# Attention on 64x64 TensorE tiles: 60-key tiles, stationary V, and a normaliser by Ln and Exp

## The chip, the cores and the metric

The kernel runs on one core of a Trainium2 chip. The time is the device time of one execution in microseconds; of three runs of the kernel before, the median is 182.83 (182.55 to 184.69).

A core has four engines that matter here, each with its own in-order queue: TensorE (PE in the profile; PEld is its weight load) multiplies matrices and writes to PSUM, VectorE (DVE) and ScalarE (ACT) work on elements, GpSimd (POOL) makes tables and issues DMAs, and SyncE (SP) issues DMAs. PSUM has eight banks here; a group of matmuls fills one or two, and DVE or ACT empties them before the next group can have them.

## The reference

Attention with a window, then a gated long convolution. B = 4, H = 8 heads, S = 768, D = 64, so 512 model columns.

```python
scores = scale * np.matmul(q, k.transpose(0, 1, 3, 2))
is_global = pos[None, :] < 8
is_local = (rel >= 0) & (rel < 96)                   # rel = query - key
keep = is_global | is_local
bias = -slopes[:, None, None] * dist                 # dist: 96 for far global keys
a = softmax(where(keep, scores + bias, -1e9))
x = (a @ v) as (B, S, 512)
proj = x @ w_proj                                    # x1, x2, x3, 512 columns each
x2_conv = irfft(rfft(x2) * rfft(filter), n=768)
out = (x1 * x2_conv * x3) @ w_out
```

Every query sees itself, the 95 keys before it, and the first eight keys.

## The kernel before

The kernel is one long program over four batches. `attention(b)` makes x transposed (`xT`, model columns on partitions), `gate` multiplies it with the outer two thirds of w_proj (L910), `conv(b)` does the middle third (L964), a Fourier transform as matmuls (L737), the product with the filter's spectrum on DVE, the inverse (L986, L989), the gating and the output projection (L1012).

**How attention is tiled.** Keys are in seven tiles of 120, each of 128 partitions with the eight global keys in front. A tile is seen by 216 queries (the last two by fewer). `transposes` brings q and k, 128 rows at a time, into `QT` and `KT` (L751). `scores` takes a pair of heads: each head's 64 rows of KT and QT are a 64-row tile of TensorE, and the two heads go to two banks (L788). ACT takes Exp of 864 columns at a time (L802), and DVE multiplies with a table of decayed and masked weights (L809); in batch 0, for two of three groups, the distances are instead added in PSUM by matmuls with `near` and `slope` (L779). `values` takes 128 columns of E as the stationary operand and 65 columns of V as the moving one, the 65th a column of ones, so that the row sums come with the result (L827, L832). The result has queries on partitions; DVE takes the reciprocal (L856) and multiplies (L851), and `transpose_x` turns it (L872) and copies it to `xT`.

**What sets the order.** A planner (`Plan`) places every operation on its engine by list scheduling: an operation's rank is its batch's due time plus a bias and a noise, costs are estimates, PSUM banks are given out as the plan goes, and an operation with two possible engines (`"AV"`) takes the earlier one. The order found is written out as the program; at run time the queues follow it and wait by semaphores. `fill` puts matmuls on an unused tile (`busy`, L419) where the plan leaves PE idle. The `table` of an ACT operation tells the planner when to add 1.3 us for a change of activation table. Batch b+1's attention is planned into the time of batch b's convolution. Loads are issued by POOL in 256-byte rows, cast to half precision on the way (L439); batch 0's q comes through SP in full precision and is cast by ACT or DVE. The SP queue also copies the global rows of V and stores the output (L1020).

Of the kernel before, what the change touches and what calls it, by code (L numbers as in the profile page):

```python
# [17 lines left out]
P = 128  # L18
NG = 8
KL = P - NG  # L20
# [40 lines left out]
class Op:  # L61
    __slots__ = ("cost", "fn", "preds", "succs", "wait", "tail", "bias", "acq", "use", "n",
                 "start", "end", "ready", "rank", "noise", "lean", "need", "eng", "bytes", "batch", "table", "name", "order", "first", "landed")


class Plan:
# [7 lines left out]
    def op(self, eng, cost, fn, r=(), w=(), acq=(), use=(), nbytes=0, table=None, name="",  # L74
           bias=0.0, after=()):
# [5 lines left out]
        o.batch, o.bias, o.n = self.batch, self.bias + bias, len(self.ops)  # L81
# [69 lines left out]
    def schedule(self):  # L151
        self.prepare()
        for seed in self.SEEDS:
            self.shake(seed)
        return self.program(self.fill(self.lay()))

    def shake(self, seed):
        r = random.Random(seed)
        if r.random() < 0.4:
            groups = sorted({(o.name, o.batch) for o in self.ops if o.eng not in "GS"})  # L160
            g, by = r.choice(groups), r.gauss(0.0, 5.0)
            lean = r.gauss(0.0, 0.3)
            for o in self.ops:
                if (o.name, o.batch) == g:
                    o.noise += by
                    o.lean += lean
            return
        share = r.choice((0.005, 0.02, 0.05))
        for o in self.ops:
            if r.random() < share:  # L170
                o.noise += r.gauss(0.0, 5.0)
                o.lean += r.gauss(0.0, 0.3)

    def lay(self):
# [8 lines left out]
        table = [None]  # L183
# [4 lines left out]
        while live:  # L188
# [25 lines left out]
            if e == "A" and o.table and table[0] != o.table:  # L214
                cost += 1.3
                table[0] = o.table
            o.start, o.eng, o.end = s, e, s + cost
# [21 lines left out]
            for x in o.succs + after.get(o, []):  # L239
# [8 lines left out]
    SEEDS = (4, 6, 12, 14, 28, 33, 52, 54, 91, 94, 109, 172, 179, 217, 284, 340, 370, 416, 512,  # L248
             1076, 1771, 1829, 3912, 4133, 4161)
    FAVOUR = 0.0  # L250
# [78 lines left out]
class Fused:  # L329
    PERIOD = 40.0  # L330
    NEAR = 2
    TWICE = frozenset((b, j, s) for b in range(4) for j in range(4) for s in range(2))
    LATER = ()
    WL = [], [], [], [(0, 256), (1024, 256), (256, 256), (1280, 256), (512, 512)]
    SHIFT = 0.0
    LONG = 0.6
    EW = [216, 216, 216, 216, 216, 168, 48]
    GRP = [(0, 1), (2, 3), (4, 5, 6)]
    Q0 = [0, 240, 480]
    QW = [240, 240, 288]  # L340

    def __init__(self, ctx, tc, q, k, v, n_global, n_local, w_proj, filt, w_out, out):
# [10 lines left out]
        self.K0 = [KL * t for t in range(6)] + [S - KL]  # L353
# [6 lines left out]
    def buffers(self):  # L360
# [5 lines left out]
        self.qn = t("qn", [P, 6, H, D])  # L366
        self.kn = t("kn", [P, 7, H, D])
        self.vn = [t(f"vn{i}", [P, 7, H, D + 1]) for i in range(2)]
        self.QT = t("QT", [P, 4, S])
        self.KT = t("KT", [P, 4, 7 * P])  # L370
        self.E = [t(f"E{i}", [P, 2, 1536]) for i in range(4)]
        self.mask = t("mask", [P, H, 648])
        self.xn = [t(f"xn{i}", [P, 2, 7, 2, D]) for i in range(2)]
# [25 lines left out]
        self.rc = [t(f"rc{i}", [P, 12], F32) for i in range(4)]  # L399
        self.dg = t("dg", [P, 264], BF16)  # L400
        self.far = t("far", [NG, 216])
        self.near = t("near", [P, 2, 480], BF16)
        self.slope = t("slope", [P, 4, 2, P], BF16)
# [4 lines left out]
        self.irow = t("irow", [1, 5, P], I32)  # L408
# [27 lines left out]
    def load(self, eng, dst, src, w, nbytes, name, r=()):  # L436
        self.loads += 1
        e = {"G": self.nc.gpsimd, "S": self.nc.sync}[eng]
        return self.g.op(eng, 0.57 + 0.00035 * nbytes[0] if eng == "G" else 0.5, lambda _: e.dma_start(dst, src),  # L439
                         w=w, r=r, nbytes=nbytes, name=name, bias=-2000.0 + self.loads)  # L440

    def load_rows(self, what, dst, src, b, t):

        lo, hi = self.K0[t], self.K0[t] + KL
        self.load("G", dst[P - (hi - lo):P, t, :, 0:self.D],
                  src[b, :, lo:hi, :].rearrange("h p d -> p h d"), [what + (t,)], (8 * (hi - lo), 256),
                  f"load{what}{t}")

    def load_run(self, what, dst, src, t, n):

        rows = src[0, :, self.K0[t]:self.K0[t] + KL * n, :].rearrange("h (t p) d -> p t h d", t=n)
        self.load("G", dst[NG:P, t:t + n, :, 0:self.D], rows, [what + (i,) for i in range(t, t + n)],
                  (8 * KL * n, 256), f"load{what}{t}")

    def load_q(self, b, t):
        src = self.q[b, :, P * t:P * t + P, :].rearrange("h p d -> p h d")
        if b == 0:
            st = self.ot[t].rearrange("p (h d) -> p h d", h=self.H)
            self.load("S", st, src, [("ot", t)], (1024, 256), f"q{t}")
            self.g.op("AV", {"A": act(512), "V": 0.7}, lambda e: self.copy(  # L460
                e, self.qn[:, t], st), r=[("ot", t)], w=[("qn", t)], name="cast")
        else:
            self.load("G", self.qn[:, t], src, [("qn", t)], (1024, 256), f"q{t}")

    def load_v(self, b, ts):
        vt, s = self.vn[b % 2], b % 2
        if b == 1 and ts[0] == 0:
            self.g.op("V", 0.2, lambda _: self.nc.vector.memset(vt[:, :, :, self.D:], 1.0),
                      w=[("vn1", s)], name="ones")
        for t in ts:  # L470
            self.load_rows(("vn", s), vt, self.v, b, t)
            if t == 0:
                self.load_global(vt, s)

    def load_global(self, vt, s):
        for c, (t, n) in enumerate(((0, 2), (2, 5))):
            self.load("S", vt[0:NG, t:t + n], vt[NG:2 * NG, 0:1].to_broadcast(
                [NG, n, self.H, self.D + 1]), [("vng", s, c)], (8 * n, 1040), "vglobal",
                r=[("vn", s, 0), ("vn1", s)])
# [7 lines left out]
    def setup(self):  # L487
# [4 lines left out]
        g.op("A", 0.2, lambda _: nc.scalar.activation(self.warm, self.warm, Act.Exp),  # L492
             r=["warm"], w=["warm"], table="exp", bias=-4000)
        def irow(_):
            p.iota(self.irow[:, 0:4], pattern=[[1, 4], [6, P]], base=0, channel_multiplier=0)
            p.iota(self.irow[:, 4], pattern=[[1, P]], base=0, channel_multiplier=0)
        g.op("G", 0.8, irow, w=["irow"], bias=-1975.0)

        def rows(_):
            v.memset(self.one, 1.0)  # L500
            for j in range(3):
                v.memset(self.cst[:, j:j + 1], 192.0 * (j + 1))
            v.tensor_copy(self.row, self.irow)
        g.op("V", 0.8, rows, r=["irow"], w=["rows"], bias=-1970)
# [3 lines left out]
        g.op("G", 0.45, ident, w=["ident"], bias=-1998.5)  # L508
        for lo, hi in ((0, 2), (2, 7)):
            g.op("V", dve(512 * (hi - lo), 4), lambda _, lo=lo, hi=hi: v.memset(self.kn[0:NG, lo:hi], 0.0),  # L510
                 w=[("kz", t) for t in range(lo, hi)], bias=-4500 if lo == 0 else -3500)
        for i in range(4):
            et = self.E[i]

            def gaps(_, et=et):
                gap = et[:, :, 0:1488].rearrange("p h (m w) -> p h m w", m=6)[:, :, :, 216:248]
                v.memset(gap, 0.0)
                v.memset(et[:, :, 1456:1536], 1.0)
            g.op("V", 0.34, gaps, w=[("E", i, c) for c in range(3)], name="gaps", bias=-3300)

    def tables(self):

        nc, g, S = self.nc, self.g, self.S
        exps = [x for x in g.ops if x.name in ("exp", "mask")]
        nf = 2.0 * math.pi / S * (1.0 - 4.0e-7)
        for a, n in enumerate((512, 256)):
            b = g.bank()
            g.op("P", 0.5 if a == 0 else 0.3, lambda _, a=a, b=b: self.angles(a, b.f32()),
                 r=["rows"], acq=[b], after=[x for x in exps if x.name == "exp"][7:8], name="angles")
# [11 lines left out]
                 r=[("th", a)], w=[("fwd", a)], table="sin", name="sines", after=exps)  # L541
# [43 lines left out]
    def distances(self):  # L585


        g, nc, NL, n = self.g, self.nc, self.NL, 216
        o = 720 - (self.S - KL)
        p, v, dg, far, mask = nc.gpsimd, nc.vector, self.dg, self.far, self.mask  # L590

        def first(_):
            for ap, w, base in ((dg[:, 0:n], n, NG), (dg[:, n:n + 48], 48, NG + o)):
                p.iota(ap, pattern=[[-1, w]], base=-base, channel_multiplier=1,
                       allow_small_or_imprecise_dtypes=True)
                for sgn, off in ((1, 0), (-1, NL - 1)):
                    if w == 48 and sgn < 0:
                        continue
                    p.affine_select(ap, ap, pattern=[[sgn, w]], base=off + sgn * base,
                                    channel_multiplier=-sgn, compare_op=Alu.is_ge, fill=-HUGE)  # L600
            p.affine_select(dg[:, n:n + 48], dg[:, n:n + 48], pattern=[[0, 48]],
                            base=-NG - o, channel_multiplier=1, compare_op=Alu.is_ge, fill=-HUGE)
# [623 lines left out]
```

## Time and profile before

| | |
|---|---|
| median of three runs | 182.83 us (182.55 to 184.69) |
| span of the profiled execution, first to last instruction | 181.1 us |
| PE busy | 170.5 us, mean granted clock 0.986 |
| DVE busy | 160.4 us |
| ACT busy | 154.1 us |
| POOL busy | 76.5 us |
| gates of batch 0, first matmul to last | 28.58 to 42.85 |
| first gate matmul of batches 1, 2, 3 | 65.04, 103.35, 140.54 |
| last output matmul fed | 177.4 |

The page has only the span of the execution that it shows; what lies around it is not in it, so the table has the runs' times beside it. Busy time is the time in which at least one instruction of an engine was under way. On PE, matmuls overlap, so how much an engine could still take is better read from the distance between starts; on ACT and DVE neighbours overlap by some 0.1 us too.

### The profile page before, as it was taken

How to read it: one execution, taken by the hardware profiler on the slowest of the kernel's cores; microseconds unless marked ns; L12 is line 12 of the kernel's file. 1: busy time of each engine (PE TensorE's matmuls, PEld its weight loads, DVE VectorE, ACT ScalarE, POOL GpSimd, SP SyncE). 2: the span in 40 equal slices, each digit the busy share in tenths (PEclk: the TensorE clock that was granted, in tenths of full speed). 3: DMA queues.
4: the chain of work that ended last, by engine and by line, in shares of the span. 5: the costliest groups of instructions: out<-in, count | busy, mean ns of one | idle time of the engine just before them, and what ended most of it. 6: DMA issues, size and time to landing. Idle time of an engine off the chain costs nothing.

```text
span 181.1 us, 4437 instructions
## 1 busy us (share of the span) xinstructions
PE 170.5 (94%) x1693; PEld 104.6 (58%) x1693; DVE 160.4 (89%) x376; ACT 154.1 (85%) x305; POOL 76.5 (42%) x97
## 2 busy tenths in 40 slices
PE   7895999999879999999999999999999999999991
PEld 2364866666445557974355759654476875447540
DVE  6828779999999999899979989999889999999960
ACT  7885899899999997797998998999789977887652
POOL 7997985279997979999400100000000000000000
PEclk9997899999999999999999999999999999999998
DMA  6999999999999999999963400000440000025135
GB/s 128 202 152 143 138 189 207 180 141 142 143 144 161 151 134 139 139 145 151 143 234 120 31 0 4 0 0 4 174 176 4 0 5 0 0 98 195 58 148 199
DMA packets 90916, 20.47 MB, mean 113 GB/s; under 512 B 83816, under 2 KB 87824, under 8 KB 90896
## 3 DMA queue, kind: packets, MB, share of 16 engines
q0 software_dynamic: 80912, 12.14, 106.4%
q1 hardware_dynamic: 9984, 8.06, 14.3%
q8 instruction: 13, 0.21, 0.5%
q14 instruction: 7, 0.06, 0.1%
HBM read 25.84 MB, written 6.29 MB: 177 GB/s over the span
## 4 chain that ended last, share of the span: by engine, by line
PE 73%; DMA 11%; ACT 7%; POOL 4%; issue 2%; DVE 1%; POOLq 0%; ACTq 0%
PE bank L910 20%; PE bank L1012 12%; PE bank L964 10%; DMA qn<-in_q_dram 7%; PE bank L737 5%; PE bank L751 5%; PE bank L986 5%; PE bank L788 4%; DMA kn<-in_k_dram 4%; PE bank L872 3%; PE bank L827 3%; ACT E L802 3%; PE bank L832 2%; POOL vn L439 1%; ACT h L427 1%
## 5 line engine op out<-in xcount | busy, mean ns | idle before, releaser
L910 PE MATMUL bank<-xT,w 128*128 128x384 f16 x256 | 43.9, 326 | 0.0
L802 ACT ACTIVATE E<-bank 128x864 f16<-128x864 f32 x48 | 41.4, 919 | 0.8 <-PE bank L788 0.4
L910 PEld LDWEIGHTS <-w 128*128 128x128 f16 x256 | 24.2, 98 | 15.4 <-DVE xT L423 0.2
L439 POOL DMA_DIRECT2D kn<-in_k_dram x28 | 25.8, 927 | 11.6 <-PE bank L751 11.4
L439 POOL DMA_DIRECT2D vn<-in_v_dram x28 | 25.8, 927 | 4.3 <-DMA vn<-in_v_dram 1.3
L809 DVE TENSOR_TENSOR E<-E,mask 128x864 f16<-128x864 f16 x40 | 23.1, 596 | 0.5 <-ACT E L802 0.5
L1012 PE MATMUL bank<-wo,y 128*128 128x512 f16 x96 | 21.9, 379 | 0.0
L439 POOL DMA_DIRECT2D qn<-in_q_dram x18 | 16.3, 912 | 6.7 <-ACT fwd L540 3.2
L851 DVE TENSOR_TENSOR xn<-bank,rc 128x512 f16<-128x512 f32 (+1 forms) x24 | 18.3, 770 | 0.3
L920 ACT CAST g<-bank 128x384 f16<-128x384 f32 x32 | 15.7, 496 | 3.2 <-PE bank L910 2.7
L827 PE MATMUL bank<-vn,E 128*128 128x65 f16 x224 | 16.1, 195 | 1.7 <-ACT E L802 1.1
L427 ACT ACTIVATE ot<-bank 128x512 f32<-128x512 f32 x22 | 12.9, 608 | 5.2 <-PE bank L1012 5.1
L827 PEld LDWEIGHTS <-E 128*128 128x128 f16 x224 | 14.5, 98 | 3.9 <-issue 1.0
L788 PE MATMUL bank<-QT,KT 64*128 64x216 f16 (+2 forms) x224 | 15.7, 242 | 1.0 <-ACT E L802 0.7
L427 ACT ACTIVATE ab<-bank 128x512 f16<-128x512 f32 x23 | 14.0, 613 | 2.8 <-PE bank L964 2.8
L427 ACT ACTIVATE x<-bank 128x384 f16<-128x384 f32 x27 | 13.7, 513 | 3.1 <-PE bank L910 2.7
L832 PE MATMUL bank<-vn,E 128*128 128x65 f16 x192 | 15.6, 194 | 0.0
L1012 PEld LDWEIGHTS <-y 128*128 128x128 f16 x96 | 9.2, 98 | 10.7 <-DVE y L1056 0.6
L423 ACT CAST eo<-bank 128x384 f16<-128x384 f32 x28 | 12.0, 513 | 2.8 <-PE bank L989 2.6
L832 PEld LDWEIGHTS <-E 128*128 128x128 f16 x192 | 13.4, 98 | 1.3 <-issue 0.7
L788 PEld LDWEIGHTS <-KT 64*128 64x128 f16 x224 | 8.4, 94 | 9.7 <-issue 6.9
L419 PE MATMUL bank<-idle 128*128 128x512 f16 x37 | 11.9, 452 | 1.2 <-DVE idle L490 1.2
(139 smaller groups left out, 363.0 us busy)
## 6 DMA issues: line engine op xcount, KB each, us to landing
out_dram<-ot SPq DMA_DIRECT2D x24, 256.0 KB, 2.0
kn<-in_k_dram POOLq DMA_DIRECT2D x28, 120.0 KB, 6.0
vn<-in_v_dram POOLq DMA_DIRECT2D x28, 120.0 KB, 7.0
qn<-in_q_dram POOLq DMA_DIRECT2D x18, 128.0 KB, 6.6
ot<-in_q_dram SPq DMA_DIRECT2D x6, 256.0 KB, 6.8
w<-in_moe_w_proj_dram POOLq DMA_DIRECT2D x4, 256.0 KB, 8.0
g<-in_moe_filter_fft_dram POOLq DMA_DIRECT2D x1, 768.0 KB, 13.6
w<-in_moe_w_proj_dram POOLq DMA_DIRECT2D x1, 512.0 KB, 10.6
```

Source lines behind the costliest of these rows:

```text
L427: self.nc.scalar.mul(out, in_, c)
L439: return self.g.op(eng, 0.57 + 0.00035 * nbytes[0] if eng == "G" else 0.5, lambda _: e.dma_start(dst, src), w=w, r=r, nbytes=nbytes, name= ...
L788: nc.tensor.matmul(bs[hh].f32()[:, off:off + w], self.KT[hs, hp, P * m:P * m + P], self.QT[hs, hp, KL * m:KL * m + w], start=(off == 0 and ...
L802: g.op("A", act(864), lambda _: nc.scalar.activation(eo, bs[0].two()[:, :, 0:432].rearrange("p h (m w) -> p h m w", m=2), Act.Exp, scale=s ...
L809: g.op("V", dve(864, 2), lambda _: nc.vector.tensor_mul(eo, eo, mk), r=[("E", hp, gi), ("mask", hp)], w=[("E", hp, gi)], name="masked")
L827: nc.tensor.matmul(o[:, n, hh], ef[:, at:at + P], vt[:, t, 2 * hp + hh, :], start=first, stop=(t == 0), skip_group_check=True)
L832: nc.tensor.matmul(o[:, n, hh], ef[:, at:at + P], vt[:, t - 1, 2 * hp + hh, :], start=False, stop=True, skip_group_check=True)
L851: nc.vector.tensor_mul(to, o[:, :, :, 0:D], rc.to_broadcast([P, 2, 2 * nt, D]))
L910: nc.tensor.matmul(bk.f32()[:, 0:h], self.w[:, c, o + P * j:o + P * j + P], self.xT[:, c, h * s:h * s + h], start=(c == 0), stop=(c == 3))
L920: g.op("A", act(h), lambda _: nc.scalar.copy(x3, pts[1].f32()[:, 0:h]), use=[pts[1]], w=[ko], name="x3")
L964: nc.tensor.matmul(bk.f32(), src[:, c], w[:, c, DM:2 * DM], start=(c == 0), stop=(c == 3))
L1012: nc.tensor.matmul(bk.f32(), y[:, c, P * t:P * t + P], self.wo[:, c, :], start=(c == 0), stop=(c == 3))
```

## The change

**Tiles.** Keys are in 13 tiles of 60, with four global keys in front: 64 partitions, seen by 156 queries. Even tiles hold the first four global keys, odd ones the other four; any two neighbours cover all eight. A pair of heads stands on partitions 0 to 63 and 64 to 127; every score matmul is a 64x64 tile, and the four tiles of TensorE are used by four matmuls in a row: two pairs of heads (banks `bs[0]`, `bs[1]`), two heads each. In one bank, one head's result goes to the upper and the other's to the lower partitions. ACT's Exp takes 936 columns at a time, eight times a batch in place of twelve.

**Values.** V (60 or 64 keys by 64 columns) is stationary and E moves, so the result has model columns on partitions: x comes out transposed, and `transpose_x`, the ones column, the reciprocal and xn are gone.

**Normaliser.** Sums over keys come from matmuls with `ones` in 32-column tiles (`norms`), for queries 0 to 359 and 360 to 767. ACT takes Ln of them and Exp of minus that; both are planned as of table "exp". The result, one row per head, is spread over 64 partitions: in batch 0 by matmuls with `pick` and a copy, afterwards by SP DMAs, eight per half. One DVE multiplication from PSUM gives `xT`.

**Batch 0 and setup.** q and k of batch 0 are loaded by POOL, two heads at a time, six rows of one head behind each other (1536 bytes), and transposed in 64-column tiles. All scores of batch 0 get their distances by matmul. The angle tables for the Fourier transform come first, ahead of attention, and the masks move behind it. V is loaded by half and pair of heads, 60 rows at a time.

**Planner.** PE operations get a mode, and a change of mode costs 0.1 us in the plan; noise and preference are read from two strings, one character per operation, in place of seeds.

The core of the diff:

```diff
 class Fused:
-    EW = [216, 216, 216, 216, 216, 168, 48]
-    GRP = [(0, 1), (2, 3), (4, 5, 6)]
+    SPLIT = 360
+    RUNS = (0, 1, 2), (3, 4, 5), (6, 7, 8), (9, 10, 11, 12)
+    OFF = 0, WIN, 2 * WIN, 2 * WIN + 108
...
+    def load_six(self, what, dst, src, hp):
+        rows = src[0, 2 * hp:2 * hp + 2].rearrange("h (p j) d -> p h (j d)", j=6)
...
+    def scores(self, j, a, near):
...
+            for m, o in zip(self.RUNS[a], self.OFF):
+                w = self.width[m]
+                for i in range(2):
+                    for x in range(2):
+                        hp, hs = 2 * j + i, slice(64 * x, 64 * x + 64)
+                        os = slice(64 * (x ^ i), 64 * (x ^ i) + 64)
+                        nc.tensor.matmul(bs[i].f32()[os, o:o + w], self.KT[hs, hp, m],
+                                         self.QT[hs, hp, KB * m:KB * m + w], start=not near, stop=True,
+                                         skip_group_check=True)
...
+    def norms(self, b, s):
...
+            for i, (m, o, a, c) in enumerate(parts):
+                for hp in range(4):
+                    nc.tensor.matmul(bk.f32()[32 * hp:32 * hp + 32, o], self.ones[:, hp % 2],
+                                     self.E[hp // 2][:, a, hp % 2, c], start=(i == 0),
+                                     stop=(i == len(parts) - 1), skip_group_check=True)
...
+        g.op("A", act(n), lambda _: nc.scalar.activation(ln, bk.f32()[:, 0:n], Act.Ln), use=[bk],
+             w=["ln"], table="exp", name="ln")
+        g.op("A", act(n), lambda _: nc.scalar.activation(r, ln, Act.Exp, scale=-1.0), r=["ln"],
+             w=[("r", s)], table="exp", name="inv den")
+        for hp in range(4):
+            if b == 0:
+                b2 = g.bank()
+                g.op("P", pe(n), lambda _, hp=hp, b2=b2: nc.tensor.matmul(
+                    b2.f32()[:, 0:n], self.pick[:, hp], r, start=True, stop=True), acq=[b2],
+                    r=[("r", s), "pick"], name="spread r")
+                g.op("AV", self.evac(n), lambda e, hp=hp, b2=b2: self.copy(
+                    e, self.rb[:, hp, lo:lo + n], b2.f32()[:, 0:n]), use=[b2], w=[("rb", hp, s)],
+                    name="rb")
+                continue
+            for x in range(2):
+                p0 = 32 * hp + 16 * x
+                self.load("S", self.rb[64 * x:64 * x + 64, hp, lo:lo + n],
+                          r[p0:p0 + 1, None, :].to_broadcast([1, 64, n]),
+                    [("rb", hp, s, x)], (64, 2 * n), "rb", r=[("r", s)])
+
+    def values(self, b, j, s):
...
+            for t, (m, o, a, c) in enumerate(parts):
+                for i in range(2):
+                    for x in range(2):
+                        ks, os = slice(64 * (x ^ i), 64 * (x ^ i) + 64), slice(64 * x, 64 * x + 64)
+                        nc.tensor.matmul(bs[i].f32()[os, o], vt[ks, m, 2 * j + i],
+                                         self.E[j][ks, a, i, c], start=(t == 0),
+                                         stop=(t == len(parts) - 1), skip_group_check=True)
...
+        g.op("V", dve(2 * n, 1, True), lambda _: nc.vector.tensor_mul(
+            self.xT[:, 2 * j:2 * j + 2, lo:lo + n], bs[0].two()[:, :, 0:n],
+            self.rb[:, 2 * j:2 * j + 2, lo:lo + n]), use=bs,
...
-        g.op("V", 0.066 + 0.025 * nt, lambda _: nc.vector.reciprocal(rc, view()[:, :, :, D:D + 1]),
-             use=bs, w=[key], name="rc")
...
-    def transpose_x(self, j, c):
```

## The prediction

> **What bounds the kernel now.** I read the busy shares first (three engines near full; the store's 2.0 us to landing is for later), then the stretches between the gate matmuls (L910) of one batch and the next, then the spacing of matmuls in the timeline and in the chain that ended last.
>
> ```profile
> PE 170.5 (94%) x1693; PEld 104.6 (58%) x1693; DVE 160.4 (89%) x376; ACT 154.1 (85%) x305; POOL 76.5 (42%) x97
> ...
> out_dram<-ot SPq DMA_DIRECT2D x24, 256.0 KB, 2.0
> ```
> Stretches between first gates of batches 1, 2 and 3 and to the end (length, busy time and number of PE, weight loads, DVE, ACT, POOL; clock, DMA share, GB/s): PE, DVE and ACT are all nearly covered, at full clock.
> ```profile
> 65.04:103.35 38.31, 37.96 (x408) 24.38 (x405) 36.09 (x75) 33.15 (x62) 23.01 (x26) 1.00 1.89 140
> 103.35:140.54 37.19, 37.15 (x389) 22.89 (x386) 34.05 (x71) 33.87 (x65) 0.00 (x0) 1.00 0.12 44
> 140.54:177.40 36.86, 36.77 (x279) 21.65 (x275) 33.98 (x76) 27.80 (x57) 0.00 (x0) 1.00 0.18 68
> ```
> The chain (start, length, what): runs of equal matmuls back to back give their spacing.
> ```profile
> 77.06 1.12 PE bank L751 x20
> 78.18 5.20 PE bank L910 x32
> ...
> 140.05 0.56 PE bank L788 x12
> ```
> The timeline (start, length to the end of the last): starts are what counts.
> ```profile
> 124.83 0.38 PE L964 MATMUL bank<-w,xo 128*128 128x512 f16 x1
> 125.14 0.36 PE L788 MATMUL bank<-QT,KT 64*128 64x216 f16 x4
> 125.43 0.60 PE L737 MATMUL bank<-ab,fwd 128*128 128x512 f16 x2
> ...
> 137.38 0.19 PE L827 MATMUL bank<-vn,E 128*128 128x65 f16 x1
> 137.41 0.19 PE L832 MATMUL bank<-vn,E 128*128 128x65 f16 x1
> ```
> A group (busy, mean ns) of 64-column tiles:
> ```profile
> L713 PE MATMUL bank<-g,fwd 128*64 128x512 f16 x8 | 1.1, 385 | 0.0
> ```
> ACT's timeline: spacing of the Exps, and a table load with what follows it.
> ```profile
> 12.25 3.24 ACT L802 ACTIVATE E<-bank 128x864 f16<-128x864 f32 x4
> ...
> 34.37 1.28 ACT L540 ACT_TABLE_LOAD   x1
> 35.66 0.94 ACT L540 ACTIVATE fwd<-y 128x512 f16<-128x512 f32 x2
> ```
> A busy PE is not a full PE (matmuls overlap), so I count spacings. 32 gates in 5.20 us: 162.5 ns for 384 columns, 0.423 ns a column. 20 transposes in 1.12 us: 56 ns. A values matmul, 65 columns: 30 ns, although its own duration is 190. Twelve score matmuls of 1728 columns would need 0.73 us in a row and took 0.56: two 64-row tiles run at once. Eight of 512 columns into 64-column tiles would need 1.7 us and took 1.1: column tiles pair too. Entering and leaving a tiled mode costs 0.1 us each: the 512-column matmul of 124.83 is done feeding at 125.05, the next starts at 125.14; four of 216 feed in 0.18 us, the next starts 0.29 later.
>
> With these prices PE needs 141.2 us from the first gate (28.58) to the last matmul (feeding until 177.4), and 148.9 passed. By stage, elapsed against PE's need: 36.5 to 31.7 (DVE, counted in the same way, needs 35.1 there), 38.3 to 37.4, 37.2 to 36.6, 36.9 to 35.5. **After the first stage PE is full, with DVE (35 to 36) close behind**; the three last stages lose 2.9 us together.
>
> **The change, engine by engine** (counts from the order of the built program).
>
> PE, four batches. Removed: 208 transposes of q and k (11.6 us), 48 slope matmuls (2.9), 224 scores (9.0), 416 values (12.4), 112 transposes of x (6.2), 67 mode changes (6.4): 48.5. Added: 144 transposes whole and 96 half-wide in pairs (10.8), slopes (1.6), 416 scores of 64x64 tiles, 59904 columns, four at once with 10 ns of stagger (7.3), 240 normaliser matmuls in 32-column tiles, four at once (3.7), 8 that spread r (1.3), 480 values (7.4), 77 mode changes (7.3): 39.4. **PE saves 9.1 us.** Four at once is not in the trace; the bounds are that (0) and pairs alone, as the rows show for either tiling (+16.3 for slopes, scores, values). I take four, since row and column pairing each show starts close together.
>
> [...]
>
> ACT, at the spacing of instructions in a row (864-element Exp: 0.77 us; 512: 0.48; 384: 0.37): 48 Exps become 32 of 936 at 0.83 (-10.4); copies of x, q, slopes, distances and tables go (-11.4); evacuations and masks -4.2; Ln and Exp of the normaliser 16 x 0.38 (+6.0); rb and gv +3.6. But the plan marks Ln as of Exp's table, and **the built program holds 19 table loads instead of 3**: each Ln has its own set, and Exp is loaded again behind it. The row at 34.37 gives 1.28 us, with the next Activate at once behind: 16 x 1.29 = +20.7. Sum +4: ACT stays at some 158 us.
>
> [...]
>
> DVE: 40 masks become 24 of 936 (-7.5), reciprocals, xn and xT go (-26.7), x comes (16 of 720 or 816 elements from PSUM at 0.82 and 0.92, from xn's 0.61 for 512: +13.9), 32 tiny copies of global keys +2.9, evacuations taken over +6.8, setup -4: **-15**. The engine that was second behind PE gets room.
>
> SP: the 24 stores get 48 broadcasts of r before or between them (batches 1 to 3, sixteen each). A store's row gives 2.0 us to land on an idle chip, an SP copy at 41.6 us, while POOL's loads ran, was issued in 0.7 to 0.85 us and its pair was down 5 us later. So eight take 4 to 5.5 us to issue and 2 to 3 to land. Behind them on SP wait only stores and global rows of V, early enough. POOL: q and k of batch 0 come in 8 loads of 1536-byte rows; at the 190 to 207 GB/s which the page shows for 512-byte writes, 1.57 MB take 8 us, so the last lands near 12 us (before: last k used at 22.6); V follows at 18, w at 27, under cover of ACT.
>
> **Start.** Gates of either half need columns 0 to 383 or beyond 360, so all of batch 0 has to be normalised. ACT's order: angle tables and Sin end at 9.5 (behind DVE's 8.6), gv, load, mask 12.5, four evacuations 15.4, seven Exps 21.2, load and Ln 22.9, load, eighth Exp and r 25.3, mask 26.0, load and Ln 27.7, rb, load, r 29.8, six rb copies 32.3; then DVE's last x, 33.5. First gate: **34** against 28.6 before. Four of its loads (5.2 us) lie in this chain in full.
>
> **Sum.** PE needs 131.5 us from the first gate on (141.2 before). 34.0 + 131.5 + 2.9 (waiting as in the last three stages) + 3.5 (tail behind the last matmul, as before) = 171.9. To it come stalls by the other 12 loads, 15.5 us of ACT: from 0 (ACT has 15% idle) to all. Per stage ACT needs 34 and 38 us against PE's 35 and 35.5, so they are not free, and the last stage has room: I take half, 7.8. Span 179.7. The profiled execution's span was 181.1 and the median of three runs 182.83, so 1.7 lie around it: **181.4 us**, 0.8% below.
>
> **Rivals.**
> A, the forecast, 0.42: 176 to 187 with the start 3 us earlier or later and a tenth to nine tenths of the loads.
> B, 0.28: the loads fall into ACT's gaps (or don't run as listed) and DVE's room takes up what is left: 171.9 + 1.7 = 174. For it: DVE's fall, 85% on ACT. Against: two stages where ACT needs as much as PE.
> C, 0.22, slower: **the normaliser's chain ends last in each batch**: Exps, Ln, load, r, load, Ln, load, r, eight SP issues, landing, x, then gates. It decides once r of the second half is later than 9 us before PE reaches the gates. In batch 1 the Exps end near 60, r near 69, x near 77; PE arrives at 69.7: 8 us. Batch 2 the same with free queues: 5; batch 3, with 24 output matmuls in between: 1.5. 14.5 in place of 7.8: span 186.4, 188 us.
> D, 0.08: sets of four run as pairs, 16.3 less 4 in batch 0, under ACT's cover: 194.
>
> From these: faster by over 2% (below 179.2, about what a measurement of this kernel can tell from no change) 0.28 + a quarter of A = 0.39; slower (above 186.5) 0.08 + 0.14 of C = 0.22; the rest 0.39. The range 172 to 190 leaves out D and the edges of B and C. For A alone: 176 to 187.
>
> **What would show it.** Start: first gate near 34, with four table loads ahead of it. Tiles: 12 score matmuls in some 0.25 us; 0.4 or more is D. Table loads: 19 of 1.28 us. C: PE idle ahead of the first gates of batches 1 and 2, released by x, x waiting for a landing of rb. DVE near 145, ACT near 158 us. Wrong would be the whole if PE had idle time of another cause (banks held by values until rb lands) or if loads of batch 1 came later than before.

## The result, and the profile after

The changed kernel takes **203.7 us** (median; 202.4 to 206.5) where the kernel before, beside it, takes 183.6: ratio 1.107, 95% interval 1.100 to 1.115. It is slower. The forecast was 181.4 with a range to 190, so the prediction was wrong; rival C named the place, and priced it too low. Ratios, differences between programs and the table of medians further down leave out runs over 1.5% above a kernel's fastest; the medians beside "Measured" are of all its runs.

The profiled execution took 202.43 us and has a span of 200.7. Its page opens with the busy shares; PEclk is the granted TensorE clock in tenths, slice by slice of 5 us.

```profile
PE 167.9 (84%) x2103; PEld 97.0 (48%) x2103; DVE 145.7 (73%) x351; ACT 158.9 (79%) x271; POOL 73.7 (37%) x97
...
PEclk9999979999999999999999799999996999999999
...
PE 41%; ACT 36%; DMA 7%; DVE 6%; SPq 4%; issue 4%; ACTq 0%; DVEq 0%
```

No engine is full any more: PE falls from 94% to 84%. The third line is the chain that ended last by engine: DMA and SP's queue together make 11% of it, for the spreading of r.

The stretches from the first gates of a batch to those of the next, and from the last such gates to the last output matmul fed (length, then busy time and number for PE, weight loads, DVE, ACT, POOL; clock, DMA share, GB/s):

```profile
35.90:83.57 47.67, 37.26 (x530) 23.31 (x530) 37.07 (x84) 37.73 (x66) 36.54 (x44) 1.00 1.94 137
83.57:127.81 44.24, 38.57 (x543) 23.14 (x542) 33.72 (x77) 39.60 (x67) 9.97 (x12) 0.96 0.94 95
127.81:166.08 38.27, 32.57 (x383) 18.48 (x383) 27.59 (x50) 29.75 (x53) 0.00 (x0) 0.96 0.36 43
166.08:197.10 31.02, 30.98 (x178) 16.49 (x177) 28.73 (x64) 21.02 (x42) 0.00 (x0) 1.00 0.28 104
```

Only the last stage, which has no next batch's attention in it, is filled by PE. The three others are 10.4, 5.7 and 5.7 us longer than PE's busy time. The list of waits (who, for what: us in all, times, longest) says for what:

```profile
DVE xT L909 <- DMA rb<-r: 11.8, 6, 3.1
...
PE bank L946 <- DVE xT L909: 7.0, 3, 2.9
```

PE's gates wait for x, and x waits for r to land on its 64 partitions. Of the 21.8 us which PE is idle in those three stretches, the list puts 10.6 down to x (7.0 of them at the gates); most of the rest are waits for what ACT makes, of at most 2.7 us a cause. What stands in front of the gates of batch 1, first in ACT's timeline (start, length to the end of the last, what), then at the end of the chain (start, length, what):

```profile
60.17 0.94 ACT L829 ACTIVATE E<-bank 128x936 f16<-128x936 f32 x1
61.13 1.28 ACT L870 ACT_TABLE_LOAD   x1
62.42 0.47 ACT L870 ACTIVATE ln<-bank 128x360 f32<-128x360 f32 x1
...
63.38 1.28 ACT L872 ACT_TABLE_LOAD   x1
64.68 0.50 ACT L872 ACTIVATE r<-ln 128x360 f16<-128x360 f32 x1
...
67.15 1.28 ACT L870 ACT_TABLE_LOAD   x1
68.44 0.51 ACT L870 ACTIVATE ln<-bank 128x408 f32<-128x408 f32 x1
68.97 1.28 ACT L872 ACT_TABLE_LOAD   x1
70.26 0.54 ACT L872 ACTIVATE r<-ln 128x408 f16<-128x408 f32 x1
```

```profile
76.76 5.62 DMA rb<-r
82.39 0.03 issue
82.42 0.05 DVEq L909
82.46 0.04 issue
82.51 1.02 DVE xT L909
83.53 0.04 issue
83.57 8.61 PE bank L946 x52
```

Four table loads of 1.28 us stand one behind the other between the last Exp (61.1) and the second r (70.8), with conv's evacuations between them. SP issues the last copy of r at 76.76, and 5.62 us pass before x may start. In batch 3, where POOL loads nothing any more, SP's sixteen copies take 13 us from the first issue to the last (2.1 of them between the halves, until the second r ends at 155.6), and the last two x wait 2.1 us each:

```profile
148.07 13.04 SPq L455 DMA_DIRECT2D rb<-r  x16
```
```profile
161.92 1.01 DVE L909 TENSOR_TENSOR xT<-bank,rb 128x816 f16<-128x816 f32 x1 [2.11 <-DMA rb<-r]
...
165.01 1.01 DVE L909 TENSOR_TENSOR xT<-bank,rb 128x816 f16<-128x816 f32 x1 [2.08 <-DMA rb<-r]
```

PE's new tiles are as cheap as forecast. PE's timeline (start, length to the end of the last):

```profile
59.39 0.40 PE L822 MATMUL bank<-QT,KT 64*64 64x156 f16 x12
59.72 0.54 PE L863 MATMUL bank<-E,ones 128*32 128x156 f16 x24
```

Twelve score matmuls and the change of mode behind them took 0.33 us; the prediction had some 0.25 and, by its own price, 0.1 for the change, and 0.4 or more as the sign of pairs.

### The profile page after: what moved, and what is told of

Read it like the earlier page. It is cut to its first block, busy times and chain, and to the rows that moved or that the text cites. A ratio compares the mean times of both kernels' runs of the same rounds, so it can differ in the third digit from the quotient of the medians.

```text
span 200.7 us, 5282 instructions
## 1 busy us (share of the span) xinstructions
PE 167.9 (84%) x2103; PEld 97.0 (48%) x2103; DVE 145.7 (73%) x351; ACT 158.9 (79%) x271; POOL 73.7 (37%) x97
## 4 chain that ended last, share of the span: by engine, by line
PE 41%; ACT 36%; DMA 7%; DVE 6%; SPq 4%; issue 4%; ACTq 0%; DVEq 0%
PE bank L946 20%; ACT E L829 11%; PE bank L1048 9%; DMA rb<-r 7%; PE bank L1000 5%; SPq L455 4%; ACT L870 4%; ACT L872 3%; DVE xT L909 3%; ACT ab L443 2%; PE bank L746 2%; ACT h L443 2%; ACT ln L870 2%; ACT X L439 2%; PE bank L435 2%
## 5 line engine op out<-in xcount | busy, mean ns | idle before, releaser
L455 POOL DMA_DIRECT2D vn<-in_v_dram x33 | 28.1, 883 | 8.4 <-PE bank L900 8.4
L829 ACT ACTIVATE E<-bank 128x936 f16<-128x936 f32 x32 | 28.8, 986 | 0.0
L909 DVE TENSOR_TENSOR xT<-bank,rb 128x720 f16<-128x720 f32 (+1 forms) x16 | 15.1, 954 | 15.8 <-DMA rb<-r 11.8
L455 POOL DMA_DIRECT2D kn<-in_k_dram x22 | 19.4, 883 | 5.1 <-PE bank L900 3.2
L842 DVE TENSOR_TENSOR E<-E,mask 128x936 f16<-128x936 f16 x24 | 15.1, 639 | 5.6 <-ACT E L829 5.4
L746 PE MATMUL bank<-ab,fwd 128*128 128x512 f16 x40 | 12.9, 427 | 4.8 <-ACT ab L443 2.7
L443 ACT ACTIVATE x<-bank 128x384 f16<-128x384 f32 x27 | 13.2, 499 | 2.8 <-PE bank L946 2.0
L443 ACT ACTIVATE ab<-bank 128x512 f16<-128x512 f32 x19 | 11.3, 609 | 3.2 <-PE bank L1000 3.2
L1022 PE MATMUL bank<-inv,X 128*128 128x256 f16 x64 | 11.5, 273 | 2.6 <-DVE xT L909 1.5
L958 DVE TENSOR_TENSOR g<-g,x 128x384 f16<-128x384 f16 x32 | 10.7, 351 | 2.9 <-ACT x L443 2.6
L822 PE MATMUL bank<-QT,KT 64*64 64x156 f16 (+2 forms) x416 | 11.1, 226 | 0.5 <-DVE xT L909 0.3
L900 PEld LDWEIGHTS <-vn 64*64 64x64 f16 x480 | 9.0, 114 | 5.2 <-issue 3.8
L900 PE MATMUL bank<-E,vn 64*64 64x156 f16 (+5 forms) x480 | 10.4, 230 | 1.2 <-ACT eo L439 0.6
```

Source lines behind the costliest of these rows:

```text
L443: self.nc.scalar.mul(out, in_, c)
L746: self.nc.tensor.matmul(b.f32(), self.fwd[:, f], src(i, t), start=(n == 0), stop=(n == len(terms) - 1))
L829: g.op("A", act(936), lambda _: nc.scalar.activation(et, bs[0].two()[:, :, 0:468], Act.Exp, scale=self.scale), use=bs, w=[("E", j, a)], ta ...
L842: g.op("V", dve(936, 2), lambda _: nc.vector.tensor_mul(eo, eo, mk), r=[("E", j, a)] + [("mask", hp) for hp in (2 * j, 2 * j + 1)], w=[("E ...
L900: nc.tensor.matmul(bs[i].f32()[os, o], vt[ks, m, 2 * j + i], self.E[j][ks, a, i, c], start=(t == 0), stop=(t == len(parts) - 1), skip_grou ...
L909: g.op("V", dve(2 * n, 1, True), lambda _: nc.vector.tensor_mul(self.xT[:, 2 * j:2 * j + 2, lo:lo + n], bs[0].two()[:, :, 0:n], self.rb[:, ...
```

## The experiments

Two theories of what stands ahead of the gates: **L**, the table loads; **S**, the spreading of r by SP. Against them: **P**, that 64x64 tiles cost PE more than counted, and later **O**, that the order, laid by a planner that believed in cheaper Ln and copies, is what is slow.

All edits are against the changed kernel. The first seven runs share the order of ACT, DVE and PE with it, so that they make a table.

### One load of a set that holds Ln and Exp

```diff
+    def both(self):
+        if not self.loaded:
+            self.loaded = True
+            self.nc.scalar.add_instruction(mybir.InstLoadActFuncSet(
+                name=self.nc.get_next_instruction_name(), engine=mybir.EngineType.Activation,
+                act_func_set_id=6, ins=[], outs=[]))
...
-            g.op("A", act(5 * n), lambda _, hp=hp: nc.scalar.activation(
+            g.op("A", act(5 * n), lambda _, hp=hp: [self.both(), nc.scalar.activation(
```

> The changed kernel with one explicit load, ahead of the first Exp, of an activation set that holds both Ln and Exp; 3 table loads in place of 19, every other instruction and the order of each engine as in the changed kernel. Theory L (the table loads are the delay): all 16 lie in the chain, four of 1.29 us ahead of the first gates and four ahead of the second r of each of batches 1 to 3, so 20.6 us go: 183. Theory S (the spreading of r by SP is the delay; its 16 copies of a batch run one behind the other at about 0.95 us each, from the first r to the last landing some 17 us in batch 1): only the two loads ahead of the FIRST r count in batches 1 to 3, so 5.1 at the start and 2.6 three times: 191. Theory P (the 64x64 tiles cost PE more than counted, and PE is the delay): 16 loads under cover, 200 to 203.

Measured: 191.9 (190.6 to 193.6), ratio to the kernel before 1.046 (1.038 to 1.054). 12.6 us go (203.4 to 190.9), as theory S said (191), not 20.6. The first gates come at 30.2 instead of 35.9, so 5.7 of it is the start, and the other twelve loads gave only 6.9: with them away the copies of r are late, and x waits 14.5 us for them.

### r from 16 partitions instead of one

The matmuls with `ones` leave every r in 16 equal rows. The copy may read any of them:

```diff
-                          r[p0:p0 + 1, None, :].to_broadcast([1, 64, n]),
+                          r[p0:p0 + 16, None, :].to_broadcast([16, 4, n]),
```

> The changed kernel with each SP copy of r reading its 64 rows from the 16 partitions that hold the same row, four each, in place of all 64 from one; as many copies, packets and bytes. Theory S1 (64 reads of one partition get in each other's way: packets of 720 bytes take 110 to 240 ns on the mean, and a copy follows the last after 0.95 us though SP issues one each 0.62): the packets fall to under 100 ns, the pace becomes the issue's 0.62, the last landing of a batch comes 3 to 5 us earlier: 190 to 196. Theory S2 (the queue's pace does not depend on where the rows come from): 202 to 205.

Measured: 199.6 (197.4 to 201.9), ratio 1.081 (1.074 to 1.088). Packets and pace are as S1 had them, the gain (5.6 us) is smaller. In the profiled run 2.2 us of it are lost ahead of the first gates, which come at 38.1 instead of 35.9 at half the TensorE clock (last section); its stages are 6.5 us shorter together. By the packets' records, the changed kernel's copies move one behind the other: eight of batch 3 were issued from 148.07 to 153.56 and moved from 149.19 to 156.46, 0.91 us each. From 16 partitions a packet takes 64 to 73 ns on the mean of a copy (70 to 257 in the changed kernel; both in batches 2 and 3), a copy moves in about 0.6 us, and the queue keeps up with the issues. But the sixteen issues stay, at 0.62 us.

### Half as many copies

```diff
-                self.load("S", self.rb[64 * x:64 * x + 64, hp, lo:lo + n],
-                          r[p0:p0 + 1, None, :].to_broadcast([1, 64, n]),
-                    [("rb", hp, s, x)], (64, 2 * n), "rb", r=[("r", s)])
+                o = self.load("S", self.rb[:, hp, lo:lo + n], r[32 * hp:32 * hp + 32, None, :].to_broadcast(
+                    [32, 4, n]), [("rb", hp, s, x)], (64, 2 * n), "rb", r=[("r", s)])
+                if x:
+                    o.fn = lambda _: None
```

One copy now brings both heads of a pair, 128 rows from 32 partitions. With the 19 loads:

> As the run beside it with all 19 table loads: the changed kernel with only the copies changed. With the loads the second r of a batch comes 5 us or more behind the first, so the first half's copies are issued by then in either form and only the second half's four issues less count: theory N 2.5 us a batch below the run with sixteen copies from 16 partitions (199.6): 191 to 194, which is also where the kernel ended that waited for no landing at all (193.1). Theory O: 198 to 201.

Measured: 193.5 (191.9 to 193.8), ratio 1.049 (1.043 to 1.056): 4.3 us less than with sixteen copies, and 2.2 above the kernel of the next run, which waits for no landing, so nearly all is had that can be had here. Of the 4.3, the profiled runs have 2.2 ahead of the first gates (38.1 against 35.9), where these copies have no part, so the gain of the number is some 2 here, where 7.5 were expected; the run with one load below shows it more clearly. By the packets' records a copy of 128 rows moves in mostly 0.7 to 0.8 us in batches 2 and 3, one of 64 rows from 16 partitions in about 0.6. The partitions of a copy were doubled with its rows; the two were not tested apart.

### No wait for the landing

```diff
-                self.load("S", self.rb[64 * x:64 * x + 64, hp, lo:lo + n],
+                self.load("S", self.rb2[64 * x:64 * x + 64, hp, lo:lo + n],
```

> Order of every engine as in the changed kernel, with its 19 table loads, Ln, Exp and SP copies; only, in batches 1 to 3 the copies of r go to a tile that nobody reads, and x is multiplied with what batch 0 spread (so those batches get batch 0's normaliser: part of the computation is left out). x waits for its values alone, not for r nor a landing. Theory W (what PE waited for ahead of the gates of batches 1 to 3, 29 us in all, is the chain through r and its landing): 175 to 180, with the first gate still at 35 to 36. Theory L (the loads hold ACT, and by it PE, whether anyone waits for r or not: 12 of them, 15.5 us, stay in the three stages): 188 to 196. Theory P (PE's tiles or an order that does not fit): above 196.

Measured: 193.1 (191.2 to 194.6), ratio 1.044 (1.038 to 1.051). Theory L's number. No x waits for a landing of r, and still the first three stages are long (columns as above):

```profile
35.90:78.60 42.70, 36.95 (x530) 23.25 (x530) 36.48 (x84) 36.66 (x64) 33.78 (x40) 1.00 1.96 138
78.60:120.50 41.90, 38.08 (x545) 23.28 (x542) 33.66 (x77) 39.12 (x70) 12.90 (x16) 0.96 1.20 113
120.50:154.90 34.40, 32.15 (x391) 18.40 (x384) 28.02 (x50) 29.72 (x53) 0.00 (x0) 0.95 0.31 24
```

The loads hold ACT, and behind them stand evacuations for the convolution (`h`, `X`), on which DVE and PE wait. The chain ahead of batch 1's gates, with the loads at L871 and L873:

```profile
66.14 0.99 ACT h L444 x2
...
67.15 1.28 ACT L871
...
68.97 1.28 ACT L873
...
70.72 0.58 ACT X L440
```

### Both at once

The set with Ln and Exp, together with no wait:

> As the run before, and the one explicit load of the set with Ln and Exp: 3 loads in place of 19. Nothing is left of the chain but the Ln and Exp themselves, in the order of the changed kernel; part of the computation is left out as there. If the chain is all that made the kernel slow: the start at 30, 131.5 us for PE, 2.9 waits, 3.5 tail, 1.7 around: 169 to 172, which is what the sum of the prediction gave without stalls (173.6, and 3.9 less by the earlier start). If the tiles cost PE more than counted: above 178.

Measured: 173.8 (172.9 to 176.6), ratio 0.947 (0.942 to 0.952). Its stages (columns as above):

```profile
29.84:69.30 39.46, 36.91 (x529) 22.78 (x529) 37.84 (x86) 31.40 (x60) 34.34 (x40) 1.00 2.18 166
69.30:106.50 37.20, 36.35 (x547) 22.09 (x545) 32.97 (x76) 33.95 (x66) 13.61 (x16) 1.00 1.39 134
106.50:136.70 30.20, 30.20 (x387) 17.94 (x384) 27.23 (x50) 24.60 (x49) 0.00 (x0) 1.00 0.39 32
136.70:167.20 30.50, 30.50 (x181) 16.60 (x178) 28.53 (x64) 21.80 (x44) 0.00 (x0) 1.00 0.39 132
```

**Theory P falls.** The last two stages are PE from end to end, and take 60.7 us; the prediction's count for them is 131.5 less 35 and 35.5, so 61.0. In the first, DVE is busy 37.8 of 39.5 us. Against the run before, with the same copies that nobody waits for, the first three stages are 12.1 us shorter: that is what the twelve loads (15.4 us of ACT) cost there without any wait for r.

With one load and sixteen copies from 16 partitions:

> The whole computation, order as in the changed kernel: one explicit load of the set with Ln and Exp, and SP's copies reading from 16 partitions. A copy then takes 0.62 us on the queue, a half 7.5 us from r to the last landing, in place of 16, 12.7 and 9.4 us with the set alone. Theory L and S1 (the two are causes of their own and add up): second r at 59.6, 105.1 and 144.7, landings at 67, 112.6 and 152.2 in place of 75.8, 117.8 and 154.1: 15 us less than with the set alone, 177 to 180. If the queue is not what is late there: 188 to 192.

Measured: 185.1 (184.8 to 185.3), ratio 1.010 (1.006 to 1.014). Between the theories; x still waits 6.3 us for landings. By the packets' records the last landing of a batch is 12.8, 11.1 and 7.8 us behind the second r, where 7.5 was expected: in batches 1 and 2 the two r now come some 3 and 2 us apart, so the second half's copies stand behind the first half's, sixteen issues in a row.

With one load and eight copies:

> The whole computation with three table loads and with eight copies of r per batch (128 rows each, from 32 partitions), every engine but SP in the order of the changed kernel. Theory N (the number: from the first r of a batch to the last landing sixteen issues take 10 us and eight take 5): 5 us a batch less than with sixteen copies from 16 partitions in this order (185.1), of which the last microseconds meet PE's own need: 174 to 178. Theory O (the order laid anew made the run of 175.4): 183 to 186.

Measured: **176.0** (175.2 to 180.7), ratio 0.956 (0.949 to 0.962): theory N. Nothing is left out here, ACT, DVE and PE do the same instructions in the same order as in the changed kernel but for the loads, and it is 4.4% faster than the kernel before. Its stages:

```profile
30.20:71.34 41.14, 37.11 (x530) 22.95 (x530) 38.19 (x86) 31.58 (x61) 34.32 (x40) 1.00 2.15 169
71.34:108.41 37.07, 36.22 (x544) 22.01 (x541) 32.38 (x75) 33.82 (x65) 13.82 (x17) 1.00 1.18 129
108.41:138.56 30.15, 30.15 (x388) 17.87 (x382) 27.16 (x50) 24.55 (x49) 0.00 (x0) 1.00 0.26 78
138.56:169.10 30.54, 30.54 (x181) 16.72 (x179) 28.64 (x64) 21.84 (x44) 0.00 (x0) 1.00 0.21 79
```

and the waits for r, which were 11.8 us:

```profile
DVE xT L917 <- DMA rb<-r: 1.4, 1, 1.4
```

The medians of these eight programs, all with the changed kernel's order (us, over the runs that the ratios compare):

| | 16 copies, one partition | 16 copies, 16 partitions | 8 copies, 32 partitions | no wait |
|---|---|---|---|---|
| 19 loads | 203.4 (the change) | 197.8 | 193.5 | 191.3 |
| 3 loads | 190.9 | 185.1 | 175.2 | 173.5 |

Each cause hides part of the other: the loads cost 12.6 us while the copies are slow and 17.9 when nobody waits for them, the copies 12.1 with the loads and 17.4 without. Together they are 30.0.

### r by matmul in every batch

```diff
-            if b == 0:
+            if True:
                 b2 = g.bank()
```

The planner lays another order here, since the operations are others. With the 19 loads:

> The changed kernel with r spread in batches 1 to 3 as it is in batch 0: eight matmuls with pick and eight copies by ACT or DVE in place of eight SP copies per half; the 19 table loads stay; the planner lays the order anew with the same strings. Theory S: the second r ends at 70.8, 116.7 and 155.6 and x follows 2.6 us later in batch 0, where it comes by matmul, in place of 11.7, 10.1 and 9.4: 9, 7.5 and 7 us less wait, 23 in all, to which PE pays some 1.3 us a batch and ACT and DVE 3: 182 to 187. Theory L: PE waits for the loads in any case, and the evacuations come on top: 196 to 203. Theory P: 204 to 208, since PE gets 3.9 us more.

Measured: 208.7 (208.2 to 208.8), ratio 1.140 (1.135 to 1.144): slower than with SP, a miss for theory S and above all three ranges. ACT's timeline ahead of batch 2's gates (126.8):

```profile
116.64 1.28 ACT L872 ACT_TABLE_LOAD   x1
117.93 0.54 ACT L872 ACTIVATE r<-ln 128x408 f16<-128x408 f32 x1
118.38 0.78 ACT L439 COPY QT<-bank 128x768 f16<-128x768 f16 x1
119.06 1.70 ACT L439 CAST rb<-bank 128x408 f16<-128x408 f32 x4
120.62 3.21 ACT L439 CAST eo<-bank 128x384 f16<-128x384 f32 x8
```

The copies out of PSUM fall to ACT, the engine with the loads, and in this order conv's evacuations (`eo`) wait behind them; the last x starts at 125.6, 7 us after r. PE's list of waits shows a second cost: the spreading matmuls stand in PE's own queue and wait for r there, 9.1 us in five waits, where the changed kernel, which spreads by matmul in batch 0 alone, has one of 1.4. How much each of the two adds was not tested by itself. With one load:

> Both edits: three table loads, r spread by matmul in all batches. Theories L and S together (the stalls of 29 us ahead of the gates of batches 1 to 3 and 5 us at the start are these two and nothing else): start at 31, PE's need of 131.5 plus 3.9 for the spreading, 2.9 waits, 3.5 tail, 1.7 around: 174 to 177, faster than the kernel before. If a third cause holds PE (the tiles, or an order laid for other costs), 185 or more.

Measured: 184.0 (182.9 to 186.7), ratio 1.006 (1.001 to 1.010), 7 us more than expected. Two tries at the rest, first without the unused matmuls:

```diff
-                if n > 0:
+                if n > 0 and o.start < 28.0:
```

> Both edits of the run with r by matmul and three loads, and the 32 unused matmuls that the plan puts into gaps that it foresees after the first gates (0.216 us each, 6.9 us; 21 of them stand between the last gates and the last output matmuls) are left out. Theory F (the gaps foreseen are not there on the chip, so these matmuls cost PE their time): 177 to 180. Theory G (PE would wait there anyway, or its clock falls without them): 183 to 187.

Measured: 184.7 (183.6 to 186.7), ratio 1.009 (1.005 to 1.013): theory G, they cost nothing. Then with the two strings looked for anew:

> Three table loads and r by matmul and copy in all batches, as in the run that gave 184.0, with the order laid anew for these operations. Theory O: 30.1 + 131.5 + 3.9 for the spreading + 2.9 + 3.5 + 1.7 = 173.6, so 172 to 177. If the order is not what was left: 182 to 186.

Measured: 181.2 (180.0 to 182.1), ratio 0.985 (0.974 to 0.996): between the theories. That order pulled attention forward until it waited for POOL's loads of k (10% of its chain), so where the matmul form would end with an order that fits was not settled.

### The order

The planner told the prices, nothing else changed, strings looked for anew by the planner's own costs:

```diff
-             w=["ln"], table="exp", name="ln")
+             w=["ln"], table="ln", name="ln")
...
+                if o.name == "rb":
+                    rbs = max(rbs, o.end + 0.6) + 0.96
+                    ready = o.landed = rbs + 0.6
```

> The operations of the changed kernel, all of them, with its 19 table loads and its sixteen one-partition copies of r per batch; only the plan is told what they cost (Ln has a table of its own, an SP copy of r takes 0.96 us behind the one before it and lands 0.6 later) and the strings that lay the order were looked for anew with these prices. Theory O (the loss is in an order laid for a shorter chain: other work could stand in the wait): the start stays at 35, PE's 131.5 and 2.9, 3.5, 1.7 around come to 175, and ACT's 20 us of loads leave it at 80% of that, so 178 to 186. Theory C (the chain of Exps, loads, r and landings can't be hidden by any order, since the next batch's scores, banks and copies hang on it): 196 to 204.

Measured: 190.2 (189.6 to 190.6), ratio 1.036 (1.028 to 1.044). Between O and C: an order that knows of the wait hides 13.2 us of it with the same operations, not all. With the causes gone, a new order has nothing to hide. Eight copies, one load:

> The whole computation with three table loads; r is spread by SP in four copies per half, each of 128 rows read from 32 partitions (four rows each), planned at 0.75 us each; order laid anew. If such a copy goes at the issue's pace (0.62 us) or up to 0.8: a half lands 5 us behind r and PE's need sets the time: 30.1 + 131.5 + 2.9 + 3.5 + 1.7 = 169.7, so 168 to 174. If 128 rows take twice what 64 from 16 partitions did (1.25 us): 174 to 179.

Measured: 175.4 (174.9 to 177.8), ratio 0.955 (0.946 to 0.964), just above the first range and the same as 176.0 in the old order. Sixteen copies from 16 partitions, one load:

> The operations of the run that gave 185.1 (one load of the set with Ln and Exp, sixteen copies of r per batch from 16 partitions each), with the order laid anew, a copy priced at 0.62 us behind the last and landing 0.6 later. Theory O (order laid for other prices is what lies between 185.1 and 175.4): 173 to 178. Theory N (half as many copies is what the faster kernel has ahead: four issues of 0.6 less per half): 180 to 184, since eight issues take 5 us and four 2.5, in each of three batches.

Measured: 186.3 (185.2 to 189.2), ratio 1.011 (1.001 to 1.021), above both ranges and no better than 185.1 in the old order. So between 185 and 175 it is the copies, half as many of twice the size, not the order.

## Why the prediction was wrong, step by step

**Where the 21 us are.** Span 179.7 forecast, 200.7 measured. The start is 1.9 later (35.9 for 34). PE's need with the waits that stay is 137.4 in place of 134.4 (the run without loads and waits, from first gate to last fed). The tail is 3.6 for 3.5. The stalls are 23.8 in place of 7.8: the four stages of the changed kernel are 8.2, 7.0, 8.1 and 0.5 us longer than those of that run. 1.9 + 3.0 + 0.1 + 16.0 = 21.0.

**The step that failed** is "stalls by the other 12 loads, 15.5 us of ACT: from 0 ... to all. ... I take half, 7.8", with SP's copies costed at nothing beside it; the runs showed 23.8 us of stalls in its place. Three things were wrong in it. It took the loads as work that spreads over ACT's gaps; they stand in ACT's queue right ahead of what PE waits for next, r and evacuations for the convolution, and with no wait for r they still cost 12.1 us. It left the copies' wait out of the sum and gave it a rival of its own (C), which took its 14.5 in place of the 7.8; the table shows two causes that both act. And the copies were mis-sized: "eight take 4 to 5.5 us to issue and 2 to 3 to land", so 6 to 8.5 from r to the last landing; by the packets' records it was 11.3, 9.6 and 8.9 in batches 1 to 3, because copies from one partition follow each other after 0.8 to 1.0 us where SP issues one each 0.62.

**C's prices** were 8, 5 and 1.5; the stalls are 8.2, 7.0 and 8.1. Its condition, the second r less than 9 us ahead of the gates, was right: from each of its own gates, at the pace of the run without loads and waits, the changed kernel would have reached the next gates at 75.4, 120.8 and 158.0, only 4.6, 4.1 and 2.4 us behind the second r, and it needs 12.8, 11.2 and 10.5 from r to the gates; the differences are the stalls. In the run without loads and waits the second r ends 10.2, 9.4 and 8.1 us ahead of the gates, so for copies this slow the order has no slack even without the loads. Batch 3's 1.5 failed on r itself, not on the copies alone: two loads stand ahead of the last Exp and two more up to r, so r is 27.8 us behind batch 2's gates, against 22.1 without.

**PE** was right where it is the fullest engine: 30.2 and 30.5 us for stages counted at 61.0 together. The first two took 39.5 and 37.2 where 35 and 35.5 were counted; in the first DVE is busy longer than PE (37.8 us to 36.9), where the prediction took PE as the one that sets the time. Four matmuls at once held: in the run of 173.8 us, 96 values matmuls (24 sets of four, 2940 columns for each of the four tiles) took 1.46 us, from 132.55 to the start of the next matmul. At 0.423 ns a column four at once need 1.24 us and pairs alone (rival D) 2.5. The 0.22 us between 1.24 and 1.46 are 9 ns a set, weight loads included.

**ACT, DVE, loads**: 158.9 us (158 forecast), 145.7 (145), 19 loads of 1.283:

```profile
L870 ACT ACT_TABLE_LOAD x8 | 10.3, 1283 | 0.1
...
L872 ACT ACT_TABLE_LOAD x6 | 7.7, 1283 | 0.1
...
L829 ACT ACT_TABLE_LOAD x2 | 2.6, 1283 | 0.0
```

All three were right, and none of them said where the time would go: the sums of an engine don't show in which chain its work stands.

**Start**: four loads lie in that chain, as said; taking them away brought the gates forward by 5.7 us (5.2 forecast). Of the 1.9 us by which the gates came later than forecast, 1.7 stand ahead of those loads: the mask ends at 14.2, not 12.5, since an evacuation of q (9.14, behind a wait of 2.0 us) went ahead of Sin (9.84).

**Rival B** (174: the loads fall into gaps "or don't run as listed") is what the kernel becomes when both causes are gone: 173.8 without the wait, 176.0 with the whole computation. The runs with three loads show that one set holds Exp and Ln, but only once the program names it: the changed kernel, which names none, has 19.

## To carry to other kernels

When a sum of busy time falls on every engine, follow the one chain that a changed stage adds from its first operation to what the fullest engine waits for, and compare its length with the slack that the order has there; loads and copies in one chain are added, not weighed against each other (30.0 us together here). Count a broadcast by DMA by its number of issues (0.62 us each here) and by how many partitions it reads from (a copy of 64 rows moved in about 0.6 us from 16 partitions, and took 0.8 to 1.0 from one). Look in the built program which activation set each function has, and name one set where a single one holds all (3 loads in place of 19 here, 12.6 us with the slow copies).

## What the runs showed of the hardware

**Rows of one partition.** Copying 512 rows of 720 bytes (half a batch's r) took the queue 7.3 us with each copy's 64 rows from one partition, and 3.5 (2.7 in batch 2) as four copies of 128 rows from 32 partitions each. The DMA view of the two stretches, first the changed kernel from 149.15 to 156.50:

```profile
DMA packets 642, 0.39 MB, mean 54 GB/s; under 512 B 128, under 2 KB 640, under 8 KB 640
...
q1 hardware_dynamic: 640, 0.37, 76.5%
```

and the kernel with one load and eight copies from 127.0 to 130.6:

```profile
DMA packets 578, 0.39 MB, mean 109 GB/s; under 512 B 64, under 2 KB 576, under 8 KB 576
...
q1 hardware_dynamic: 576, 0.37, 48.7%
```

The share is of the time of 16 DMA engines: 90 us of engine time (0.765 x 16 x 7.35) for the same bytes that took 28 (0.487 x 16 x 3.6). The eight copies of the first stretch followed each other after 0.9 us. Why a packet takes longer out of one partition (70 to 257 ns on the mean of a copy, 64 to 73 out of 16) was not shown.

**One activation set for two functions** was loaded by hand and stayed loaded: from the load at 11.93 on, every Exp, Ln and copy of the run of 176.0 us goes without another, 3 loads of 1.283 us in all.

**The clock.** The changed kernel has stretches of 3.4 us at half the TensorE clock from 27.3, 112.7 and 150.2 us on, where PE had been waiting (2.9 us up to 27.08, 1.9 up to 112.56, 0.8 up to 150.04; the 7, 7 and 6 in the PEclk row), and none behind the wait of 2.9 us that ends at 83.57; the profiled runs of 173.8 and 176.0 us have none. The profiled run with sixteen copies from 16 partitions and 19 loads has one of 10.2 us, from 28.1 to 38.3, right ahead of its first gates (the 8, 5 and 5 of its row):

```profile
PEclk9999985599999999999999987999996999999998
```

In the changed kernel the clock is back at 1.00 from 30.8 to the gates. The same matmuls, from the spreading of the second r (32.3 in both) to the first gate, take 5.8 us and 3.6. So some of the stalls can be the clock's, where PE is the last to be ready: in the changed kernel's batch 3, four 512-column matmuls of the chain (from 150.53) take 1.86 us, where four output matmuls of 512 columns, from 154.05 on at the full clock, take 0.86 from start to start. What all these stretches cost together was not measured.
